# Product 3 of the output layer by seven smaller products, in chunks 3 to 7 of an attention and GELU kernel

## The chip, the cores and the metric

One core of a Trainium2 chip. The metric is the device time of one execution in microseconds; the kernel before takes 256.05 us (median of 3 runs, 256.01 to 256.41). The engines are named as the profile names them: PE (TensorE, matmuls), PEld (its weight loads), DVE (VectorE), ACT (ScalarE), POOL (GpSimd) and SP (SyncE, which only issues DMAs here).

## The reference

Linear attention over 8 batches, 8 heads, 576 positions and 64 features, then one layer with GELU:

```python
q_s = exp(q - max) / sum over the features;  k_s = exp(k - max) / sum over the positions
kv = einsum('bhsd,bhse->bhde', k_s, v)
x = einsum('bhsd,bhde->bhse', q_s, kv), heads side by side   # 4608 x 512
g = gelu(x @ w_in)                                           # 4608 x 2048
out = g @ w_out                                              # 4608 x 512
```

Inputs and output are f32 in memory. The kernel computes its matmuls in bf16 with f32 sums.

## The kernel before, in words

**Chunks.** The 4608 rows are done in nine chunks of 512. Chunks 0 to 7 are the first 512 positions of each batch; chunk 8 collects the 64 that are left of each. The loop at L1099 runs chunks 2 to 8. In each, `h_waves` (L462) computes g from x and w_in, and `y_phase` (L673; `y_last` for chunk 8) computes the output from g and w_out. Work for later chunks is put between: `next_x` (L1088) makes x of chunk c+1 and the k·v product of chunk c+2.

**Seven products instead of eight.** Both layers split their two matrices in halves both ways, and multiply sums of quarters: seven products instead of eight. In the output layer the quarters are: rows of the chunk (LO, HI: 256 each), the inner 2048 (UP, DN: 8 tiles of 128 each) and output columns (two times 256). `y_operands` (L661) lists what each of the seven multiplies. Product 3 is g[UP, LO] times (w_out[UP, right] - w_out[DN, right]); the weight difference was written over wo_bf[UP, right] before (`mix_wo`, L877). It takes 16 matmuls with 128 x 128 of g as the weights that are loaded and 256 columns of w_out moving.

**Order of y_phase.** The order in which instructions are written is the order in each engine's queue; engines meet only by semaphores. TensorE does products 4, 3, 5, 1, 2, 6, then x and k·v for later chunks, then product 7. Between them `after(i)` calls functions that the caller hooked in. ScalarE copies product 4 to `f` (`zeros32`, L706), does the exponentials of q of chunk c+2 (hook 8), copies product 3 to c12 (L709), then the exponentials of k (hook 9). VectorE subtracts product 5 from f, sums the exponentials of q (`q_sums`, L258, hook 1) and goes on with the outputs c12, c22, c11. GpSimd waits until VectorE's last sums of g are done (`touch_g`, L1083), then casts v of chunk c+2 in four pieces (L190), scales q (`q_scale`, L266) and does two adds on c22 (L732, L733). Then y is stored and the next q, k and v are loaded, all by SP's queue in this order.

**Order of h_waves.** Four groups (q = 0 to 3) of two tiles; seven products each. `x_sums` (L444) are the sums of x that products 5, 6, 7 and 4 multiply: t1 and t2 are made at the end of the y_phase before (t1 before the k·v scaling, t2 behind it), t3 and t4 within the wave, t3 just ahead of `e_sum` of groups 0 and 1. `e_sum` (L511) adds product 6 to product 5 in PSUM and frees product 7 to go on in the same bank; `r_sum` (L514) follows it. `gelu` (L517) writes g. At the end `s_parts` (L385) makes the sums of g that the output products 5, 1, 2, 6 and 7 multiply.

**Buffers.** `vf` is the f32 landing buffer of v, two in turn. `y_sb` holds the output of half a chunk, two in turn. `quad_t` holds t1 to t4. PSUM has eight banks, whose roles rotate from chunk to chunk (`turn_roles`, L456); product 3 has a bank of its own, `bx`.

Of the kernel before, what the change touches and what calls it, by code (L numbers as in the profile page):

```python
# [8 lines left out]
FP32 = mybir.dt.float32  # L9
# [7 lines left out]
def kernel(  # L17
# [16 lines left out]
    nc = tc.nc  # L34
# [53 lines left out]
    HT = M // 2  # L88
    HN = DM // 2
    w7 = singles.tile([128, HK, HN], BF16)  # L90
    s12 = singles.tile([128, HK, M], BF16)
    s5 = singles.tile([128, HK, HT], BF16)

# [10 lines left out]
    def load_main(b, name, t, parts=1):  # L104
# [5 lines left out]
        for i in range(parts):  # L110
            nc.sync.dma_start(out=f[:, i * n:(i + 1) * n, :], in_=src[:, i * n:(i + 1) * n, :])

    def load_pair(b, name, t, parts=1):
        f = f32in.tile([128, HP, NS * D], FP32, tag=name + "f")
        st[b][name + "f"] = f
        src = t[b].rearrange("h (p n) d -> (h p) (n d)", n=NS).rearrange("(x q) f -> q x f", q=128)
        n = HP // parts
        for i in range(parts):
            h0 = i * n
            if b == 0 and name == "k" and i == 0:  # L120

                nc.scalar.dma_start(out=f[:, 0, :], in_=src[:, 0, :])
                h0 = 1
            nc.sync.dma_start(out=f[:, h0:(i + 1) * n, :], in_=src[:, h0:(i + 1) * n, :])
# [8 lines left out]
    def load_v1(i):  # L133

        if i == 0:
            st[1]["vf"] = f32in.tile([128, HP, NS * D], FP32, tag="vf", name="f")
        src = v[1].rearrange("h (p n) d -> (h p) (n d)", n=NS)
        nc.sync.dma_start(out=st[1]["vf"][:, i, :], in_=src[i * 128:(i + 1) * 128, :])

# [319 lines left out]
        roles.update(bb=r["x3"], ba=r["kv1"], x0=r["bb"], x1=r["kv0"], x2=r["x0"], x3=r["ba"],  # L459
                     kv0=r["x1"], kv1=r["x2"])  # L460

    def h_waves(c, mid):  # L462

# [50 lines left out]
        def r_sum(q):  # L514
            tt(held["r", q], held["A", q], held["r", q])
# [10 lines left out]
        if mid:  # L526
            seed(1)
            mm(1, 2, 3)
            mm(2, 0, 1)
            gelu("C", 0, 1)  # L530
            mm(5, 0, 1)
            p5_copy(0, scopy)
            p5_copy(1, scopy)
            x_sums(c, (3, 4))
            seed(2, vcopy)
            seed(3, vcopy)
            mm(6, 0, 1)
# [24 lines left out]
            gelu("r", 2, 3)  # L562
            mm(3, 2, 3)
            mm(4, 2, 3)
        else:
            mm(5, 0, 1)
            seed(1)
            p5_copy(0, scopy)
            p5_copy(1, scopy)
            mm(6, 0, 1)  # L570
            x_sums(c, (3,))
            e_sum(0)
            e_sum(1)
            x_sums(c, (4,))
            mm(2, 0, 1)
            gelu("C", 0, 1)
            mm(7, 0, 1)
            r_sum(0)
            r_sum(1)
            mm(3, 0, 1)  # L580
            for q in (2, 3):
                mm(5, q)
                mm(1, q)
            mm(4, 0, 1)
            gelu("r", 0)
            gelu("B", 0, 1)
            gelu("r", 1)
            seed(2)
            seed(3)
            gelu("A", 0, 1)  # L590
            p5_copy(2, vcopy)
            p5_copy(3, vcopy)
            s_parts(c, 0, 4, (3,))
            mm(6, 2, 3)
            e_sum(2)
            e_sum(3)
            s_parts(c, 0, 4, (4,))
            mm(2, 2, 3)
            gelu("C", 2, 3)
            mm(7, 2, 3)  # L600
            r_sum(2)
            r_sum(3)
            gelu("r", 2, 3)
            mm(3, 2, 3)
            mm(4, 2, 3)
        gelu("A", 2, 3)
        gelu("B", 2, 3)
        s_parts(c, 0, 4, (0,))
        if mid:
            s_parts(c, 0, 4, (4,))  # L610
        s_parts(c, 0, 4, (2,))
        s_parts(c, 4, 4, (0,))
        s_parts(c, 4, 4, (3,))
        s_parts(c, 4, 4, (4,))
        turn_roles()
# [54 lines left out]
        }  # L670
        return act, wgt

    def y_phase(c, ins):  # L673

        act, wgt = y_operands(c)
        if c == 1:
            at = {"bd": 3, "be": 4, "bb": 0, "bx": 1, "ba": 2}
        else:  # L680
            at = {"bd": roles["x0"], "be": roles["x1"], "bb": roles["bb"], "bx": roles["x2"], "ba": roles["ba"]}
        bd, be, bb, bx, ba = (bank(at[n], "y" + n[1]) for n in ("bd", "be", "bb", "bx", "ba"))
        ysb = [moe_sb.tile([128, 2, DM], FP32, tag="y_sb", name="y_sb", bufs=2) for i in range(2)]
        c11, c12 = ysb[0][:, :, 0:HN], ysb[0][:, :, HN:DM]
        c21, c22 = ysb[1][:, :, 0:HN], ysb[1][:, :, HN:DM]
        f = zeros32

        def two(ps):
            return ps.rearrange("p (j n) -> p j n", j=2)

        def mm(m, ps, first):
            for j in range(2):
                for k in range(HK):
                    nc.tensor.matmul(  # L694
                        ps[:, j * HN:(j + 1) * HN], act[m][:, k, j * 128:(j + 1) * 128],
                        wgt[m][:, k, :], start=(first and k == 0 and j == 0),
                        stop=(k == HK - 1), skip_group_check=True,
                    )

        def after(i):  # L700
            for fn in ins.get(i, []):
                fn()

        mm(4, bd, True)
        if c > 1:
            nc.scalar.copy(out=f, in_=bd)  # L706
            after(8)
            mm(3, bx, True)
            nc.scalar.copy(out=c12, in_=two(bx))  # L709
            after(9)  # L710
        else:
            nc.vector.tensor_copy(out=f, in_=bd)
        after(0)
        mm(5, be, True)
        after(7)
        tt(f, f, be, ALU.subtract)
        after(1)
        if c > 1:
            tt(c12, c12, two(be))
        mm(1, ba, True)  # L720
        tt(c22, two(f), two(ba))
        after(2)
        mm(2, bd, False)
        nc.scalar.copy(out=c21, in_=two(bd))
        after(3)
        if c == 1:
            mm(3, be, False)
            nc.scalar.copy(out=c12, in_=two(be))
        after(4)
        mm(6, bb, True)  # L730
        tt(c22, c22, two(bb))
        tt(c22, c22, c12, eng=nc.gpsimd)  # L732
        tt(c22, c22, c21, ALU.subtract, eng=nc.gpsimd)  # L733
        after(5)
        mm(7, ba, False)
        tt(c11, two(f), two(ba))
        y_store(c, 1, ysb[1])
        y_store(c, 0, ysb[0])
        after(6)

    def y_last(c):

# [304 lines left out]
    for t in range(4):  # L1047
# [4 lines left out]
    mix_wo(1, 1)  # L1052
    mix_wo(3, 1)
    quad["r"] = wst.tile([128, 4, 2, HT], FP32, tag="w2", name="r")
    quad["t"] = wst.tile([128, 4, 2, HT], BF16, tag="w3", name="quad_t")
    h1 = {p + 3: [lambda p=p: cast_v(2, p, nc.scalar)] for p in range(HP)}
    h1[1] = [sums[0]]
    h1[3] += sums[1:3]
# [3 lines left out]
    exp_q(2, parts=2)  # L1062
    exp_k(2)

    y_phase(1, {
        0: [sums[3]],
        7: [lambda: norm_q(2, 0, 2)],
        1: [lambda: norm_q(2, 1, 2, nc.vector)],
        2: [lambda: cast_v_all(3), lambda: xbar_step(2), lambda: exp_q(3)],
        3: [lambda: kv_step(2), lambda: exp_k(3), lambda: q_sums(3)],  # L1070
        4: [lambda: table(AF.Gelu)],
        6: [lambda: load(4), lambda: x_all(2, (3, 4, 1, 5)),
            lambda: kv_step(3, lambda: x_sums(2, (1,))), lambda: x_sums(2, (2,))],
    })

    def q_late():


        nc.gpsimd.tensor_copy(out=scr[:, 2:3], in_=quad["r"][:, 0, 0, 0:1])
        q_scale(3, nc.gpsimd)  # L1080
        xbar_step(3)

    def touch_g(c):  # L1083

# [14 lines left out]
    for c in range(2, B + 1):  # L1099
        nb = c + 2  # L1100
        if 2 < c and nb < B:
            load(nb)
        elif nb == B:
            load_qrest()
        h_waves(c, q_late if c == 2 else None)
        s_parts(c, 4, 4, (2,))
        yi = {}
        if nb <= B:
            yi[8] = [lambda: exp_q(nb)]
            yi[1] = [lambda: norm_q(nb)]  # L1110
            yi[3] = [lambda: table(AF.Gelu)]
        if nb < B:
            yi[9] = [lambda: exp_k(nb)]
            yi[0] = [lambda: touch_g(c), lambda: cast_v_all(nb)]
        if c < B:
            yi[5] = [lambda: next_x(c, nb)]
            y_phase(c, yi)
        else:
            y_last(c)

# [29 lines left out]
```

## Time and profile before

| | us |
|---|---|
| median of 3 runs (range) | 256.05 (256.01 to 256.41) |
| the profiled execution, its own time | 256.13 |
| its span, first to last instruction | 254.3 |
| PE busy | 247.7 (97%) |
| DVE busy | 209.0 (82%) |
| ACT busy | 189.1 (74%) |
| POOL busy | 67.3 (26%) |
| a steady chunk, from one product 4 to the next (110.67 to 136.48 in the chain) | 25.81 |

A timeline line gives the start in us from the span's start, the duration in us, the engine, the source line, the operation, output <- inputs by the program's names, shapes, and how many were merged (x16); in brackets the idle time before it and what ended it. Merged rows last from the first start to the last end. A matmul's duration has the pipeline in it, so sixteen matmuls of 0.272 us each take 1.91 us as a row and 1.75 us in the chain, which counts from end to end. The next operation of VectorE or ScalarE starts some 0.1 us before the last one's end. The granted clock was 1.000 throughout.

### The profile page before, as it was taken

What the parts mean: (1) busy time and instruction counts of PE and PEld (TensorE: products, weight loads), DVE (VectorE), ACT (ScalarE), POOL (GpSimd) and SP (SyncE); (2) the same over time, 40 slices, a digit from 0 to 9 for tenths busy, and PEclk for the clock granted to TensorE, in tenths of its full rate; (3) what the DMA queues carried; (4) which work ended last, traced back from release to release, by engine and by line L of the source; (5) the groups of instructions that cost most, each with busy time, mean ns of one, the idle gap of its engine ahead of it and who ended that gap; (6) DMA issues with size and microseconds to landing.
All of it is one profiled execution on the core that took longest, in us unless ns stands there. A gap on an engine that the chain in (4) does not pass through costs nothing.

```text
span 254.3 us, 6526 instructions
## 1 busy us (share of the span) xinstructions
PE 247.7 (97%) x2672; PEld 195.8 (77%) x2678; DVE 209.0 (82%) x365; ACT 189.1 (74%) x321; POOL 67.3 (26%) x64
## 2 busy tenths in 40 slices
PE   7899999999999999999999999999999999999994
PEld 3444444448888888888888888888888888888883
DVE  1878799888986989897889888988898889578972
ACT  4785988699977995899689968896886787158711
POOL 1530023000735067006700580059000900040000
PEclk9999999999999999999999999999999999999999
DMA  7999999994439935980499049904830340012033
GB/s 237 400 387 425 402 406 400 398 411 174 85 125 330 266 68 131 321 340 1 109 303 377 4 85 326 378 0 86 263 71 0 84 166 3 0 55 115 1 82 86
DMA packets 43166, 50.23 MB, mean 198 GB/s; under 512 B 20224, under 2 KB 30464, under 8 KB 42880
## 3 DMA queue, kind: packets, MB, share of 16 engines
q1 hardware_dynamic: 42416, 49.13, 57.7%
q10 hardware_dynamic: 720, 0.69, 1.0%
q8 instruction: 21, 0.34, 0.6%
q14 instruction: 9, 0.07, 0.1%
HBM read 36.70 MB, written 9.44 MB: 181 GB/s over the span
## 4 chain that ended last, share of the span: by engine, by line
PE 93%; DMA 4%; ACTq 0%; issue 0%; DVE 0%; POOL 0%
PE qa L497 19%; PE ps L377 11%; PE ya L694 10%; PE qb L497 10%; PE yd L694 10%; PE ye L694 6%; PE ps L637 5%; PE qc L497 5%; PE yb L694 5%; PE yx L694 4%; PE kv L225 2%; DMA touch<-in_moe_w_in_dram 2%; DMA f<-in_v_dram 2%; PE ps L343 2%; PE ya L764 1%; PE yd L764 1%
## 5 line engine op out<-in xcount | busy, mean ns | idle before, releaser
L497 PEld LDWEIGHTS <-quad_s 128*128 128x128 bf16 x448 | 43.8, 98 | 5.3 <-issue 0.2
L694 PEld LDWEIGHTS <-g 128*128 128x128 bf16 x448 | 43.2, 98 | 5.8 <-issue 0.4
L269 POOL TENSOR_TENSOR e<-e,recq 128x2048 bf16<-128x2048 bf16 (+1 forms) x9 | 27.4, 3046 | 72.9 <-DVE recq L264 47.7
L694 PEld LDWEIGHTS <-s 128*128 128x128 bf16 x336 | 32.9, 98 | 3.8
L497 PEld LDWEIGHTS <-wi_bf 128*128 128x128 bf16 x336 | 32.8, 98 | 3.9
L497 PE MATMUL qa<-quad_t,quad_s 128*128 128x256 bf16 x224 | 29.4, 272 | 0.0
L377 PE MATMUL ps<-xT,wi_bf 128*128 128x512 bf16 x124 | 27.8, 379 | 0.2
L428 POOL TENSOR_TENSOR y_sb<-y_sb 128x512 f32<-128x512 f32 x14 | 19.5, 1390 | 24.2 <-DVE y_sb L428 21.3
L263 DVE TENSOR_REDUCE qsum<-e 128x16 f32<-128x1024 bf16 (+1 forms) x12 | 20.9, 1743 | 4.8 <-ACT e L173 4.8
L377 PEld LDWEIGHTS <-wi_bf 128*128 128x128 bf16 x128 | 12.3, 97 | 15.2 <-issue 0.5
L428 DVE TENSOR_TENSOR qb<-qa,r 128x512 f32<-128x512 f32 x28 | 18.1, 694 | 5.8 <-ACT g L521 3.1
L505 ACT COPY qc<-qa 128x512 f32<-128x512 f32 x26 | 13.9, 577 | 12.0 <-PE qa L497 11.5
L383 ACT ACTIVATE g<-ps 128x512 bf16<-128x512 f32 x32 | 17.6, 603 | 6.1 <-PE ps L377 5.8
L173 ACT ACTIVATE e<-f 128x512 bf16<-128x512 f32 (+1 forms) x42 | 20.5, 556 | 1.9 <-DMA f<-in_q_dram 1.8
L521 ACT ACTIVATE g<-r 128x512 bf16<-128x512 f32 x28 | 17.3, 631 | 6.2 <-DVE r L428 6.2
L521 ACT ACTIVATE g<-qc 128x512 bf16<-128x512 f32 x28 | 15.2, 594 | 7.7 <-PE qc L497 7.7
L428 DVE TENSOR_TENSOR r<-qa,r 128x512 f32<-128x512 f32 x28 | 18.0, 685 | 0.9 <-PE qa L497 0.7
L402 DVE TENSOR_TENSOR s<-g 128x1024 bf16<-128x1024 bf16 x28 | 18.6, 686 | 0.0
L190 POOL CAST v_aug<-f 128x576 bf16<-128x576 f32 x25 | 17.2, 723 | 3.6 <-DMA f<-in_v_dram 3.6
L178 ACT ACTIVATE ek<-f 128x2304 bf16<-128x2304 f32 (+1 forms) x10 | 17.3, 1735 | 0.5 <-DMA f<-in_k_dram 0.5
L521 ACT ACTIVATE g<-qb 128x512 bf16<-128x512 f32 x28 | 15.1, 594 | 0.7 <-PE qb L497 0.7
L497 PE MATMUL qb<-quad_t,quad_s 128*128 128x256 bf16 x112 | 15.5, 272 | 0.0
(101 smaller groups left out, 469.3 us busy)
## 6 DMA issues: line engine op xcount, KB each, us to landing
out_dram<-y_sb SPq DMA_DIRECT2D x16, 512.0 KB, 3.4
f<-in_k_dram SPq DMA_DIRECT2D x6, 1152.0 KB, 10.0
f<-in_v_dram SPq DMA_DIRECT2D x6, 1152.0 KB, 11.7
f<-in_q_dram SPq DMA_DIRECT2D x6, 1024.0 KB, 8.1
w<-in_moe_w_in_dram SPq DMA_DIRECT2D x6, 512.0 KB, 8.7
f<-in_v_dram SPq DMA_DIRECT2D x8, 288.0 KB, 6.3
f<-in_q_dram SPq DMA_DIRECT2D x4, 512.0 KB, 8.9
w<-in_moe_w_out_dram SPq DMA_DIRECT2D x2, 1024.0 KB, 12.3
```

The costliest lines, as they stand in the source:

```text
L173: nc.scalar.activation(out=dst[:, i], in_=src[:, u], func=AF.Exp)
L178: nc.scalar.activation(out=ek[b % 2][:, i:i + n], in_=st[b]["kf"][:, i:i + n].rearrange("p x (n d) -> p x n d", n=NS), func=AF.Exp,)
L190: eng.tensor_copy(out=o, in_=i)
L263: nc.vector.reduce_sum(out=qsum, in_=st[b]["eq"][:, :, i * w:(i + 1) * w, :], axis=AX.X)
L269: eng.tensor_tensor(out=e, in0=e, in1=st[b]["recq"].unsqueeze(3).to_broadcast([128, J, w, D]), op=ALU.mult,)
L377: nc.tensor.matmul(ps, wi_bf[:, dm, t * 128:(t + 1) * 128], st[c]["xT"][:, dm, :], start=(dm == 0), stop=(dm == NDM - 1),)
L383: nc.scalar.activation(out=st[c]["g"][:, t, :], in_=ps, func=AF.Gelu)
L402: tt(out=s12[:, a, half], in0=g[:, a, half], in1=g[:, b, hi], op=ALU.add)
L428: eng.tensor_tensor(out=out, in0=in0, in1=in1, op=op)
L497: nc.tensor.matmul(held[kind, q][:, u], w, mov[m][:, k], start=(m in (1, 5) and u == 0 and k == 0), stop=(k == 1), skip_group_check=True,)
L521: nc.scalar.activation(out=g[:, t:t + 2, half], in_=held[kind, q], func=AF.Gelu)
L694: nc.tensor.matmul(ps[:, j * HN:(j + 1) * HN], act[m][:, k, j * 128:(j + 1) * 128], wgt[m][:, k, :], start=(first and k == 0 and j == 0), ...
```

## The change

In chunks 3 to 7, product 3 is itself split into halves all three ways and done by seven products ("sets") of an eighth of its work. A set has four matmuls: 128 rows of g loaded as weights, 128 columns of w_out moving, over four of the eight inner tiles. Four sets add into the same PSUM bank in 128-column blocks.

- The sums of w_out that the sets need are made once, by GpSimd: two in y_phase of chunk 1, four operations in the wave of chunk 2, behind the scaling of q.
- The sums of g (`rows`, `diag`, `cols`) are made by VectorE in every chunk: three operations within the wave, behind r_sum of groups 0 and 1, three at its end, among `s_parts`, whose order changes a little.
- Sets 4, 5 and 1 go ahead of product 4; ScalarE copies their three blocks of 128 columns out (`snap`) before it copies product 4; sets 2, 3, 6 and 7 take the place of product 3 and add on the same bank.
- The blocks are put together by six GpSimd operations of 128 x 128 f32: `corner` behind the touch of g, `corner2` behind the first cast of v (it reads c12), then the three other casts of v; `spread` on c12 ahead of the adds on c22.
- v of chunks 4 to 7 has one landing buffer instead of two; the other holds the sums.
- Hooks 4 and 6 of y_phase of chunk 1 are renamed 10 and 4.

```diff
+    def v_buf(b):
+        i = b % 2 if b < 4 else 0
+        return f32in.tile([128, HP, NS * D], FP32, tag=f"vf{i}", name="f", bufs=1)
...
             r_sum(0)
             r_sum(1)
+            if sums:
+                sums(c, 0)
...
+        if sums:
+            sums(c, 1)
+        else:
+            s_parts(c, 0, 4, (0,))
...
+        def weights(self, part):
+            W = wo_bf[:, UP, HN:DM].rearrange("p (a h b) n -> p h a b n", h=2, b=2)
+            b11, b12, b21, b22 = (W[:, i, :, :, j:j + 128] for i in range(2) for j in (0, 128))
...
+            if part == 0:
+                tt(o[0], b11, b22, eng=eng)
+                tt(o[1], b12, b22, ALU.subtract, eng=eng)
+                return
+            tt(o[2], b21, b11, ALU.subtract, eng=eng)
+            tt(o[3], b11, b12, eng=eng)
+            tt(o[4], b21, b22, eng=eng)
+            w = self.w[:, 4]
+            eng.tensor_scalar(out=w, in0=w, scalar1=-1.0, scalar2=None, op0=ALU.mult)
+
+        def sums(self, c, a):
+            A = st[c]["g"][:, UP, LO]
...
+            tt(self.rows[:, o], A[:, k1], A[:, k2])
+            tt(self.diag[:, o], A[:, k1, lo], A[:, k2, hi])
+            if a:
+                s_parts(c, 0, 4, (0,))
+            tt(self.cols[:, k], A[:, k, hi], A[:, k, lo], ALU.subtract)
+            if a:
+                s_parts(c, 4, 4, (0,))
+                s_parts(c, 0, 4, (2,))
+
+        def mm(self, c, ps, sets, first):
...
+                for i, k1 in enumerate((0, 1, 4, 5)):
+                    k2 = k1 + 2
+                    lhs, rhs, r = {
+                        1: (self.diag[:, i], self.w[:, 0, i], 0),
+                        2: (self.rows[:, i, hi], W[:, k1, lo], 2),
+                        3: (A[:, k1, lo], self.w[:, 1, i], 1),
+                        4: (A[:, k2, hi], self.w[:, 2, i], 2),
+                        5: (self.rows[:, i, lo], W[:, k2, hi], 1),
+                        6: (self.cols[:, k1], self.w[:, 3, i], 3),
+                        7: (self.cols[:, k2], self.w[:, 4, i], 0),
+                    }[m]
...
+        def snap(self, ps):
+            nc.scalar.copy(out=two_d, in_=ps[:, 0:384])
+
+        def corner(self):
+            eng, d = nc.gpsimd, self.d
+            tt(d[:, 2], d[:, 2], d[:, 1], ALU.subtract, eng=eng)
+            tt(d[:, 0], d[:, 0], d[:, 2], eng=eng)
+
+        def corner2(self, o):
+            eng, d = nc.gpsimd, self.d
+            tt(d[:, 0], d[:, 0], o[:, 0, 128:HN], eng=eng)
+            tt(d[:, 0], d[:, 0], o[:, 1, 0:128], ALU.subtract, eng=eng)
+
+        def spread(self, o):
+            tt(o[:, 0, 0:128], o[:, 0, 0:128], self.d[:, 2], eng=nc.gpsimd)
+            tt(o[:, 1, 128:HN], o[:, 1, 128:HN], self.d[:, 0], eng=nc.gpsimd)
...
+        if p3:
+            p3.mm(c, bx, (4, 5, 1), True)
+            p3.snap(bx)
         mm(4, bd, True)
         if c > 1:
             nc.scalar.copy(out=f, in_=bd)
             after(8)
-            mm(3, bx, True)
+            if p3:
+                p3.mm(c, bx, (2, 3, 6, 7), False)
+            else:
+                mm(3, bx, True)
             nc.scalar.copy(out=c12, in_=two(bx))
             after(9)
...
         after(0)
+        if p3:
+            p3.corner2(c12)
+        after(6)
         mm(5, be, True)
...
         tt(c22, c22, two(bb))
+        if p3:
+            p3.spread(c12)
         tt(c22, c22, c12, eng=nc.gpsimd)
...
-        2: [lambda: cast_v_all(3), lambda: xbar_step(2), lambda: exp_q(3)],
+        2: [lambda: cast_v_all(3), first_weights, lambda: xbar_step(2), lambda: exp_q(3)],
...
         q_scale(3, nc.gpsimd)
         xbar_step(3)
+        y3.weights(1)
...
+        p3 = y3 if 2 < c < B else None
+        h_waves(c, q_late if c == 2 else None, p3 and p3.sums)
...
-            yi[0] = [lambda: touch_g(c), lambda: cast_v_all(nb)]
+            cv = [lambda hp=hp: cast_v(nb, hp, nc.gpsimd) for hp in range(HP)]
+            yi[0] = [lambda: touch_g(c)] + ([p3.corner] if p3 else []) + cv[:1]
+            yi[6] = cv[1:]
+        elif p3:
+            yi[0] = [p3.corner]
```

More of the change, by code (lines that the diff above doesn't have):

```diff
@@ L90 @@
     w7 = singles.tile([128, HK, HN], BF16)
+    two_d = singles.tile([128, 384], FP32)
     s12 = singles.tile([128, HK, M], BF16)
@@ L111, in load_main @@
             nc.sync.dma_start(out=f[:, i * n:(i + 1) * n, :], in_=src[:, i * n:(i + 1) * n, :])
+    def v_buf(b):
+        i = b % 2 if b < 4 else 0
+        return f32in.tile([128, HP, NS * D], FP32, tag=f"vf{i}", name="f", bufs=1)
     def load_pair(b, name, t, parts=1):
-        f = f32in.tile([128, HP, NS * D], FP32, tag=name + "f")
+        f = v_buf(b) if name == "v" else f32in.tile([128, HP, NS * D], FP32, tag=name + "f")
         st[b][name + "f"] = f
@@ L135, in load_v1 @@
         if i == 0:
-            st[1]["vf"] = f32in.tile([128, HP, NS * D], FP32, tag="vf", name="f")
+            st[1]["vf"] = v_buf(1)
         src = v[1].rearrange("h (p n) d -> (h p) (n d)", n=NS)
@@ L460, in turn_roles, with h_waves @@
                      kv0=r["x1"], kv1=r["x2"])
-    def h_waves(c, mid):
+    def h_waves(c, mid, sums=None):
         h_begin(c)
@@ L607, in h_waves @@
         gelu("B", 2, 3)
[L608 to L612, printed above, removed]
+        if sums:
+            sums(c, 1)
+        else:
+            s_parts(c, 0, 4, (0,))
+            if mid:
+                s_parts(c, 0, 4, (4,))
+            s_parts(c, 0, 4, (2,))
+            s_parts(c, 4, 4, (0,))
         s_parts(c, 4, 4, (3,))
@@ L671, in y_operands, with __init__ @@
         return act, wgt
-    def y_phase(c, ins):
+    class Two:
+        def __init__(self):
+            t = f32in.tile([128, 9, 512], BF16, tag="vf1", name="two", bufs=1)
+            self.w = t[:, 0:5].rearrange("p i (k n) -> p i k n", k=4)
+            self.rows = t[:, 5:7].rearrange("p i (k n) -> p (i k) n", k=2)
+            self.cols = t[:, 7:9].rearrange("p i (k n) -> p (i k) n", k=4)
+            self.diag = quad["diag"]
+            self.d = two_d.rearrange("p (i n) -> p i n", i=3)
+        def weights(self, part):
+            W = wo_bf[:, UP, HN:DM].rearrange("p (a h b) n -> p h a b n", h=2, b=2)
+            b11, b12, b21, b22 = (W[:, i, :, :, j:j + 128] for i in range(2) for j in (0, 128))
+            o = [self.w[:, i].rearrange("p (a b) n -> p a b n", b=2) for i in range(5)]
+            eng = nc.gpsimd
+            if part == 0:
[9 more added lines that the diff above has]
+            A = st[c]["g"][:, UP, LO]
+            k, k1, k2 = slice(4 * a, 4 * a + 4), slice(4 * a, 4 * a + 2), slice(4 * a + 2, 4 * a + 4)
+            o = slice(2 * a, 2 * a + 2)
+            lo, hi = slice(0, 128), slice(128, HT)
+            tt(self.rows[:, o], A[:, k1], A[:, k2])
[4 more added lines that the diff above has]
+            if a:
+                s_parts(c, 4, 4, (0,))
+                s_parts(c, 0, 4, (2,))
+        def mm(self, c, ps, sets, first):
+            A, W = st[c]["g"][:, UP, LO], wo_bf[:, UP, HN:DM]
+            lo, hi = slice(0, 128), slice(128, HT)
+            for m in sets:
+                for i, k1 in enumerate((0, 1, 4, 5)):
[9 more added lines that the diff above has]
+                    }[m]
+                    nc.tensor.matmul(
+                        ps[:, r * 128:(r + 1) * 128], lhs, rhs,
+                        start=(first and m == sets[0] and i == 0), stop=(i == 3),
+                        skip_group_check=True,
+                    )
+        def snap(self, ps):
[11 more added lines that the diff above has]
+            tt(o[:, 1, 128:HN], o[:, 1, 128:HN], self.d[:, 0], eng=nc.gpsimd)
@@ L677, in y_phase @@
+    def y_phase(c, ins, p3=None):
         act, wgt = y_operands(c)
@@ L728, in y_phase @@
             nc.scalar.copy(out=c12, in_=two(be))
-        after(4)
+        after(10)
         mm(6, bb, True)
         tt(c22, c22, two(bb))
+        if p3:
+            p3.spread(c12)
         tt(c22, c22, c12, eng=nc.gpsimd)
@@ L738, in y_phase @@
         y_store(c, 0, ysb[0])
-        after(6)
+        after(4)
     def y_last(c):
@@ L1054 @@
     quad["r"] = wst.tile([128, 4, 2, HT], FP32, tag="w2", name="r")
-    quad["t"] = wst.tile([128, 4, 2, HT], BF16, tag="w3", name="quad_t")
+    quad["t"] = wst.tile([128, 5, 2, HT], BF16, tag="w3", name="quad_t")
+    quad["diag"] = quad["t"][:, 4].rearrange("p i (k n) -> p (i k) n", k=2)
     h1 = {p + 3: [lambda p=p: cast_v(2, p, nc.scalar)] for p in range(HP)}
@@ L1063, with first_weights @@
     exp_k(2)
+    y3 = None
+    def first_weights():
+        nonlocal y3
+        y3 = Two()
+        y3.weights(0)
     y_phase(1, {
@@ L1068 @@
         1: [lambda: norm_q(2, 1, 2, nc.vector)],
-        2: [lambda: cast_v_all(3), lambda: xbar_step(2), lambda: exp_q(3)],
+        2: [lambda: cast_v_all(3), first_weights, lambda: xbar_step(2), lambda: exp_q(3)],
         3: [lambda: kv_step(2), lambda: exp_k(3), lambda: q_sums(3)],
-        4: [lambda: table(AF.Gelu)],
-        6: [lambda: load(4), lambda: x_all(2, (3, 4, 1, 5)),
+        10: [lambda: table(AF.Gelu)],
+        4: [lambda: load(4), lambda: x_all(2, (3, 4, 1, 5)),
             lambda: kv_step(3, lambda: x_sums(2, (1,))), lambda: x_sums(2, (2,))],
@@ L1104 @@
             load_qrest()
-        h_waves(c, q_late if c == 2 else None)
+        p3 = y3 if 2 < c < B else None
+        h_waves(c, q_late if c == 2 else None, p3 and p3.sums)
         s_parts(c, 4, 4, (2,))
@@ L1113 @@
             yi[9] = [lambda: exp_k(nb)]
-            yi[0] = [lambda: touch_g(c), lambda: cast_v_all(nb)]
+            cv = [lambda hp=hp: cast_v(nb, hp, nc.gpsimd) for hp in range(HP)]
[3 more added lines that the diff above has]
+            yi[0] = [p3.corner]
         if c < B:
             yi[5] = [lambda: next_x(c, nb)]
-            y_phase(c, yi)
+            y_phase(c, yi, p3)
         else:
```

## Prediction

> **What bounds the kernel now.** I read the table of engines first, then the chain of work that ended last, then the timeline of one whole chunk.
>
> ```profile
> PE 247.7 (97%) x2672; PEld 195.8 (77%) x2678; DVE 209.0 (82%) x365; ACT 189.1 (74%) x321; POOL 67.3 (26%) x64
> ```
>
> TensorE works 97% of the span. Its chain in chunk 3 has no gap, and the last product of the kernel shows a short form:
>
> ```profile
> 110.67 1.75 PE yd L694 x16
> 112.42 1.75 PE yx L694 x16
> 114.16 1.75 PE ye L694 x16
> ...
> 249.84 0.91 PE ya L764 x16
> ```
>
> Each step starts where the last ended: TensorE alone sets the time from 58 us on, so a product is worth what it takes, if nothing else becomes late. Product 3 is `yx`: 16 matmuls of 256 columns in 1.747 us, 109.2 ns each. The last line is 16 matmuls of 128 columns, each with a weight load of its own; from first start to last start they take 0.0555 us each.
>
> What could become late is read in the stretch between chunks 3 and 4:
>
> ```profile
> 119.42 3.62 POOL L269 TENSOR_TENSOR e<-e,recq 128x2048 bf16<-128x2048 bf16 x1 [1.76 <-ACT ek L178]
> ...
> 122.99 0.42 DVE L428 TENSOR_TENSOR quad_t<-xT 128x512 bf16<-128x512 bf16 x1
> 123.00 2.94 POOL L428 TENSOR_TENSOR y_sb<-y_sb 128x512 f32<-128x512 f32 x2
> ...
> 124.13 0.69 DVE L428 TENSOR_TENSOR quad_t<-xT,quad_t 128x512 bf16<-128x512 bf16 x1
> 124.74 0.67 DVE L428 TENSOR_TENSOR y_sb<-zeros,ya 128x512 f32<-128x512 f32 x1
> ...
> 125.34 0.89 DVE L428 TENSOR_TENSOR quad_t<-xT 128x512 bf16<-128x512 bf16 x1
> ...
> 125.83 1.04 PE L497 MATMUL qa<-quad_t,quad_s 128*128 128x256 bf16 x8
> 126.54 1.30 DVE L428 TENSOR_TENSOR qb<-qa,r 128x512 f32<-128x512 f32 x2 [0.31 <-PE qa L497]
> ...
> 127.58 1.04 PE L497 MATMUL qa<-quad_t,quad_s 128*128 128x256 bf16 x8
> ```
>
> The `quad_t` rows are x_sums (1), (2), (3): one shape, 0.42, 0.69 and 0.89 us. The long ones end 0.29 us after a GpSimd add ends: 124.82 after 124.53 (123.00 and the 1.53 that the first of the two shows where it is listed alone), 126.23 after 125.94. So **a VectorE operation with two inputs in SBUF waits for the GpSimd operation that is running.** It holds for the scaling of q too:
>
> ```profile
> 35.13 1.90 POOL L269 TENSOR_TENSOR e<-e,recq 128x1024 bf16<-128x1024 bf16 x1 [19.88 <-DVE recq L264]
> ...
> 36.39 1.73 DVE L269 TENSOR_TENSOR e<-e,recq 128x1024 bf16<-128x1024 bf16 x1
> ```
>
> The VectorE row ends at 38.12, 1.09 after GpSimd's 37.03; the same row started at 64.81, as GpSimd ended, takes 1.23 in all. Operations that read PSUM (0.69 f32) show no such stretch. Today x_sums (1) starts at 122.99, just as the 3.62 us scaling ends. The two e_sums (126.54) then end at 127.84, and the second half of product 7 starts at 128.02: slack 0.18. Chunk 7 has no slack:
>
> ```profile
> 203.47 1.28 DVE L428 TENSOR_TENSOR qb<-qa,r 128x512 f32<-128x512 f32 x2
> 204.21 1.19 PE L497 MATMUL qa<-quad_t,quad_s 128*128 128x256 bf16 x8
> ```
>
> 1.19 instead of 1.04: TensorE stood for 0.15.
>
> **The change, part by part.** My sum is against the profiled execution, 256.13 us (span 254.3 and 1.8 around it); the median of the runs is 256.05.
>
> *TensorE.* Seven sets of four 128-column matmuls: 28 × 0.0555 = 1.554 for 1.747. Gain 0.193 a chunk, five chunks: **-0.97**. Nearest row above: the weight load's own duration, 98 ns, if nothing hid it: 28 × 0.098 = 2.74, a loss of 1.0 a chunk. I take 55.5, since the row has just this form.
>
> The Trainium skill ("TensorE: Matmul & The Clock Gate", Back-to-back issue gap) speaks against the change: 81 ns is what it gives for sustained pairs of load and 128-column matmul, 56 only for an isolated gap. By the 81 ns, an estimate, a chunk would lose 28 × 81 - 1747 = 0.52 us. The trace's 16 pairs in a row agree with the 56; no run so far shows 28.
>
> *Waits of the new products.* Sets 5 and 1 need the sums `rows` and `diag`. VectorE comes to them at 109.84, needs about 0.34 and 0.21 by the rows of 512 and 256 elements (0.42 and 0.28, each with the next starting 0.08 before its end), and is done by 110.5; TensorE wants them at 110.73 and 110.95. The second group of sets (2, 3, 6, 7) must not write before ScalarE's snap of 384 columns has read. ScalarE is free at 112.41 (its GELU pair of 111.45 plus 0.96); between the copies of 256 (0.38) and 512 (0.58) I take 0.48, so 112.89 plus a signal; TensorE is there at 110.51 + 0.67 + 1.75 = 112.93. I cost it 0.02 a chunk, **+0.1**; each 0.1 us that the GELUs come later costs 0.1.
>
> *VectorE.* Six operations, 0.9 us in the wave and 0.9 at its end. Idle times of 0.46, 0.18 and 0.52 us take the first, the 1.16 before `zeros` (116.02) the second. Cost nothing; without that cover up to 0.9 a chunk.
>
> *GpSimd.* Six f32 operations of 128x128 a chunk. The trace has none: above it is the 128x512 add (1.33, half of the undisturbed pair of 2.67 at 224.55), below the 128x1 cast (0.19). From the bf16 rows (1.90 for 1024, 3.62 for 2048) a fixed 0.18; then 0.18 + 128 × 2.25 ns = 0.46, of which I take 0.41 from start to start. Queued behind them are three casts of v, the scaling of q and the two adds of `y_sb`. Matters of layout come to nothing: with one buffer for v from chunk 4 on, its load is issued around 129.2 + 2 and the last cast before it is over by 121. The weight sums: two in the GpSimd idle time of 2.38 before 70.77 (512 elements, 0.18 + 512 × 1.68 ns = 1.04 each), four after 80.28, with GpSimd idle until 90.43; they can hold VectorE's sums of chunk 2 for up to 0.4, whose product 5 has 0.6 slack.
>
> *What is late next.* In chunk 3's clock: product 4 now ends 0.67 later, so the f copy (112.45) starts at 113.12, the exponentials of q end at 117.2 (116.54), c12 is copied by 117.7. GpSimd's corner2 waits for c12: 117.75 to 118.6; three casts (0.62 each) to 120.45; then the scaling, **120.45 to 124.07**, where it ran 119.42 to 123.04. TensorE meanwhile is 0.19 earlier. x_sums (1) comes at about 122.95, waits to 124.07, is done at 124.36, still ahead of product 5 (124.96 - 0.19 = 124.77). After 0.81 of k·v work x_sums (2) comes at 125.09. GpSimd has done the two spreads and begins the first `y_sb` add at about 125.0. This is a tie, and it decides.
>
> If VectorE goes first, x_sums (2) is done at 125.5, in time for product 6 (125.64). x_sums (3) comes at 126.0 and waits for the add (126.58), the e_sums end at 127.5 and 128.1 where product 7 wants them at 127.39 and, with the first wait, 127.9: **+0.28**. This falls on the waves of chunks 4, 5 and 6. Chunk 7, without casts, gets the scaling 0.6 later instead of 1.0: I take +0.3 (0 to 0.5).
>
> Sum: 256.13 - 0.97 + 0.10 + 3 × 0.28 + 0.30 = 256.40, less 0.08 for the median: **256.3**.
>
> **Rivals.** A measurement of this kernel tells about 0.2%, 0.5 us, from no change.
>
> *A, the forecast: the gain is eaten by the next wave's sums.* 255.8 to 257.0, as GpSimd's small operation is 0.43 to 0.55. Chance 0.37.
>
> *B, slower: GpSimd's add goes first at the tie.* Then x_sums (2) waits to 126.33 and product 6 stands 0.98; x_sums (3) waits for the second add (127.75), the e_sums end at 128.65 and 129.25, and product 7 stands about 0.4 more: 1.4 in each of three waves. 256.05 - 0.87 + 4.2 + 0.3 = 259.7. It decides when the add takes hold before 125.09: for it, the 0.46 of an operation puts the start at 125.0; against it, the row at 123.00 took 0.2 to get going, as x_sums (1) was under way. Down to 258.5 with shorter operations. Chance 0.31.
>
> The Trainium skill ("SBUF — State Buffer", Who interferes with whom) says that whichever of the two starts first has the shared ports for the whole instruction. The rows above agree on the whole instruction; who starts first at the tie they cannot show, and by the start times alone this would be B.
>
> *C, the gain stands.* If GpSimd's operation is nearer to 0.19 than to 0.46, the scaling starts as q's sums are ready, 120.03, and the gaps between spreads and adds let x_sums through: 256.05 - 0.97 + 0.1 = 255.2, up to 255.5 with one short stall. For it: VectorE has 0.35 to 1.5 us of slack at each x_sums. Against it: even so the scaling ends 0.6 later than now, and the e_sums have 0.18. Chance 0.24.
>
> *D, 128-column matmuls do not hide their loads.* At 98 ns, 256.05 + 5 × 1.0 = 261. The row of 55.5 speaks against it. Chance 0.04. The rest (0.04) is a late cast before k·v, whose second half has 1.3 us of slack: slower.
>
> **The numbers.** Faster by over 0.2% (below 255.54): C and a little of A, 0.26. Within: most of A, 0.26. Slower: the rest of A (0.09), B, D and the cast: 0.48. Likeliest 256.3, its own range 255.8 to 257.0. For 8 in 10 the range takes in C and most of B: 255.3 to 260.0.
>
> **What would show it.** Right: 28 matmuls of 128 columns in 1.55 us; q's scaling about 1 us later against product 4's start; `quad_t` rows of 1 us and more; gaps of TensorE before L497's products 6 and 7 in chunks 4 to 7, none in chunk 3. Wrong: `quad_t` rows at 0.42 and a period of 25.6 us instead of 25.8 (C), or no gap but slow matmuls (D). A GpSimd row of 128x128 far from 0.46 moves everything.

## The result and the profile after

| | before | after |
|---|---|---|
| median of 4 runs (range), us | 256.19 (256.01 to 256.41) | 257.87 (257.78 to 258.63) |
| the profiled execution, its own time | 256.13 | 257.78 |
| its span | 254.3 | 255.7 |
| one chunk, from one product 4 or first set to the next: chunks 3, 4, 5 | 25.80, 25.76, 25.75 | 26.12, 26.20, 26.13 |
| the same, chunks 6, 7 | 25.28, 25.22 | 25.48, 25.06 |

The changed kernel takes 1.0072 of the time before (95% interval 1.005 to 1.0093): 0.7% more, where 256.3, no difference, was forecast. The time lies in the range given, above the forecast A's own range (255.8 to 257.0) and below rival B's (258.5 to 259.7). The table of engines after:

```profile
PE 248.8 (97%) x2732; PEld 195.7 (77%) x2738; DVE 221.5 (87%) x395; ACT 190.9 (75%) x326; POOL 89.8 (35%) x100
```

GpSimd has 22.5 us more work and VectorE 12.5, and TensorE is as full as before. The chain of the work that ended last (start, time from end to end, engine, tile, line) shows in chunk 3 what the small products cost, and in the wave behind it (wave 4, the wave of chunk 4) what the rest does:

```profile
110.84 0.67 PE yx L743 x12
111.51 1.75 PE yd L789 x16
113.25 0.91 PE yx L743 x16
...
125.15 1.05 PE qb L503 x8
...
127.07 0.87 PE qc L503 x8
127.94 1.15 PE qa L503 x8
```

The 28 small matmuls take 0.67 + 0.91 = 1.58 us, product 3 took 1.75. Eight matmuls of the wave take 0.87 when nothing holds them, so products 5 (125.15) and 7 (127.94) lost 0.18 and 0.28. The timeline of the same stretch says to whom:

```profile
118.01 0.99 POOL L434 TENSOR_TENSOR two_d<-two_d,y_sb 128x128 f32<-128x128 f32 x2
118.94 1.88 POOL L196 CAST v_aug<-f 128x576 bf16<-128x576 f32 x3
...
120.78 3.62 POOL L275 TENSOR_TENSOR e<-e,recq 128x2048 bf16<-128x2048 bf16 x1
...
123.13 1.56 DVE L434 TENSOR_TENSOR quad_t<-xT 128x512 bf16<-128x512 bf16 x1
...
124.80 0.29 DVE L252 TENSOR_TENSOR kvc<-kv,rec 128x128 bf16<-128x128 f32 x1
...
125.14 1.64 PEld L503 LDWEIGHTS <-quad_s 128*128 128x128 bf16 x16 [0.30 <-DVE kvc L252]
...
125.41 0.41 DVE L434 TENSOR_TENSOR quad_t<-xT,quad_t 128x512 bf16<-128x512 bf16 x1
125.49 2.88 POOL L434 TENSOR_TENSOR y_sb<-y_sb 128x512 f32<-128x512 f32 x2
...
126.34 0.90 DVE L434 TENSOR_TENSOR quad_t<-xT 128x512 bf16<-128x512 bf16 x1
...
127.90 1.19 PE L503 MATMUL qa<-quad_t,quad_s 128*128 128x256 bf16 x8
```

The scaling of q (L275) runs from 120.78 to 124.40; before it ran 119.42 to 123.04. x_sums (1), the first `quad_t` row, takes 1.56 us instead of 0.42 and ends at 124.69, 0.29 after the scaling. The two halves of the k·v scaling (`kvc`) stand behind it on VectorE, and the weight load of product 5 waited for the first of them (124.80 + 0.29 = 125.09): this product writes into the bank that the k·v scaling still reads. Before, the same row ended 1.15 ahead of product 5 (123.81, 124.96):

```profile
123.52 0.29 DVE L246 TENSOR_TENSOR kvc<-kv,rec 128x128 bf16<-128x128 f32 x1
...
124.96 1.04 PE L497 MATMUL qb<-quad_t,quad_s 128*128 128x256 bf16 x8
```

In the changed kernel, x_sums (2) then starts at 125.41, 0.08 ahead of GpSimd's add (125.49); x_sums (3) falls into that add, takes 0.90, and product 7 is late.

In the wave of chunk 7 the adds alone do it:

```profile
203.50 2.68 POOL L434 TENSOR_TENSOR y_sb<-y_sb 128x512 f32<-128x512 f32 x2
203.62 1.42 DVE L434 TENSOR_TENSOR quad_t<-xT 128x512 bf16<-128x512 bf16 x1
...
205.71 1.19 PE L503 MATMUL qa<-quad_t,quad_s 128*128 128x256 bf16 x8 [0.21 <-DVE qb L434]
```

x_sums (3) comes 0.12 after the first add and takes 1.42, and product 7 starts 0.37 late and stands 0.15 more in its middle.

### The profile page after: what moved, and what is told of

It is laid out like the page before. It is cut to its first block, busy times and chain, and to the rows that moved or that the text cites. A ratio compares the mean times of both kernels' runs of the same rounds, so it can differ in the third digit from the quotient of the medians.

```text
span 255.7 us, 6732 instructions
## 1 busy us (share of the span) xinstructions
PE 248.8 (97%) x2732; PEld 195.7 (77%) x2738; DVE 221.5 (87%) x395; ACT 190.9 (75%) x326; POOL 89.8 (35%) x100
## 4 chain that ended last, share of the span: by engine, by line
PE 83%; DVE 6%; DMA 4%; ACT 2%; issue 2%; ACTq 0%; POOL 0%; DVEq 0%
PE qa L503 19%; PE ps L383 11%; PE qb L503 10%; PE yd L789 8%; PE ya L789 7%; PE ps L648 5%; PE qc L503 4%; PE ye L789 4%; PE yb L789 3%; PE yx L743 2%; DMA f<-in_v_dram 2%; DMA touch<-in_moe_w_in_dram 2%; DVE qsum L269 2%; DVE y_sb L434 2%; PE kv L231 1%
## 5 line engine op out<-in xcount | busy, mean ns | idle before, releaser
L275 POOL TENSOR_TENSOR e<-e,recq 128x2048 bf16<-128x2048 bf16 (+1 forms) x9 | 27.4, 3046 | 49.7 <-DVE recq L270 49.1
L789 PEld LDWEIGHTS <-g 128*128 128x128 bf16 x368 | 35.2, 98 | 4.8 <-issue 0.4
L434 POOL TENSOR_TENSOR y_sb<-y_sb 128x512 f32<-128x512 f32 x14 | 18.9, 1351 | 3.7 <-issue 2.8
L408 DVE TENSOR_TENSOR s<-g 128x1024 bf16<-128x1024 bf16 x28 | 19.8, 726 | 0.0
L1201 POOL CAST scr<-g 128x1 f32<-128x1 bf16 x4 | 0.7, 187 | 49.5 <-DVE g L411 49.5
```

The costliest lines, as they stand in the source:

```text
L275: eng.tensor_tensor(out=e, in0=e, in1=st[b]["recq"].unsqueeze(3).to_broadcast([128, J, w, D]), op=ALU.mult,)
L408: tt(out=s12[:, a, half], in0=g[:, a, half], in1=g[:, b, hi], op=ALU.add)
L434: eng.tensor_tensor(out=out, in0=in0, in1=in1, op=op)
L789: nc.tensor.matmul(ps[:, j * HN:(j + 1) * HN], act[m][:, k, j * 128:(j + 1) * 128], wgt[m][:, k, :], start=(first and k == 0 and j == 0), ...
```

## The experiments

All are compared with runs of the kernel before on the same chip (medians 256.39, 256.32 and 256.47 in the three batches), with 4 to 11 runs each. "Chunk periods" run from the start of one chunk's output layer to that of the next, from chunk 3 on.

**Without the scaling.** This kernel leaves the scaling of q by its sums out in chunks 3 to 6. The theory: what the small products save stands in full, and the loss is GpSimd's scaling of q, which now runs into x_sums.

```diff
-            yi[1] = [lambda: norm_q(nb)]
+            yi[1] = [lambda: norm_q(nb) if nb < 5 else q_sums(nb)]
```

> The changed kernel, with the scaling of q by its sums left out on GpSimd in chunks 3 to 6 (the sums are still made). Theory (GpSimd holds the SBUF reads that x_sums needs): x_sums (1) takes 0.42 instead of 1.6 us, product 5 of the next wave no longer stands 0.2 to 0.3, product 7 no longer 0.28; the chunk period falls from 26.1 to about 25.65, the time from 257.9 to 255.7 (255.4 to 256.2). Rival ScalarE (product 4 and the exponentials come 0.8 later and push VectorE's queue): nothing of that is touched, so 257.5 or more. Rival VectorE (its six added sums make it late): 257.5 or more.

Measured 255.67 us (255.46 to 256.14), ratio 0.9976 (0.9967 to 0.9985). Its timeline:

```profile
123.12 0.56 DVE L434 TENSOR_TENSOR quad_t<-xT 128x512 bf16<-128x512 bf16 x1
...
124.95 1.04 PE L503 MATMUL qb<-quad_t,quad_s 128*128 128x256 bf16 x8
...
127.58 1.04 PE L503 MATMUL qa<-quad_t,quad_s 128*128 128x256 bf16 x8
```

x_sums (1) is short, products 5 and 7 come on time and run 1.04 us. The periods are 25.65, 25.60, 25.59, 24.97, 25.06: against before, 0.16 less in each chunk, and in chunk 6 another 0.15, as the old stall of product 7 is gone. So the small matmuls bring 0.16 a chunk net, and what the changed kernel has above these periods is stall: 0.47, 0.60, 0.54 and 0.51.

**Without the corner operations.** This kernel does not put product 3's blocks together. The theory: six GpSimd operations of 128 x 128 are part of what makes the scaling late, ScalarE's later exponentials the rest.

```diff
-            yi[0] = [lambda: touch_g(c)] + ([p3.corner] if p3 else []) + cv[:1]
+            yi[0] = [lambda: touch_g(c)] + cv[:1]
...
-        if p3:
-            p3.corner2(c12)
...
-        if p3:
-            p3.spread(c12)
```

> The changed kernel with the six GpSimd operations on 128x128 blocks (corner, corner2, spread) left out in chunks 3 to 7, so product 3's blocks are not put together; snap stays. Theory: the scaling of q starts as its sums are ready, near 120.2 instead of 120.8 in chunk 3's clock, x_sums (1) waits 0.6 less, the adds come 1.6 earlier; product 5 no longer stands, product 7 stands about 0.1: 256.5 (256.0 to 256.9). Rival ScalarE: the wait for the exponentials alone already makes x_sums late, and without GpSimd's operations at least two thirds of the loss stay: 257.2 or more. Rival VectorE: 257.5 or more.

Measured 256.87 us (256.49 to 257.18), ratio 1.0021 (1.0013 to 1.003). In its timeline GpSimd stands idle ahead of the scaling: this waits for ScalarE's exponentials and q's sums, and no longer for GpSimd's own queue.

```profile
120.23 3.62 POOL L275 TENSOR_TENSOR e<-e,recq 128x2048 bf16<-128x2048 bf16 x1 [1.28 <-ACT ek L184]
...
123.14 1.00 DVE L434 TENSOR_TENSOR quad_t<-xT 128x512 bf16<-128x512 bf16 x1
...
201.29 2.87 POOL L434 TENSOR_TENSOR y_sb<-y_sb 128x512 f32<-128x512 f32 x2
...
201.72 1.30 DVE L434 TENSOR_TENSOR quad_t<-xT,quad_t 128x512 bf16<-128x512 bf16 x1
...
203.08 1.05 PE L503 MATMUL qa<-quad_t,quad_s 128*128 128x256 bf16 x8 [0.27 <-DVE quad_t L434]
```

The scaling comes 0.55 earlier than in the changed kernel, 0.63 later than before against the start of y_phase. Products 5 and 6 of waves 4 to 6 come on time; only product 7 stands, and the periods are 0.17, 0.23 and 0.24 above those of the kernel without the scaling. The lines from 201 us show rival B's mechanism where the gap is wide enough: the adds start 0.43 ahead of x_sums (2), which takes 1.30, and product 6 stands 0.44. With product 7's wait, chunk 6's period is 25.83, 0.86 above that of the kernel without the scaling, where the changed kernel has 0.51. So leaving these operations out helps waves 4 to 6 and hurts wave 7.

**The k·v scaling first.** The theory: product 5 waits for the bank that the k·v scaling reads.

```diff
-            kv_step(nb, lambda: x_sums(c + 1, (1,)))
-            x_sums(c + 1, (2,))
+            kv_step(nb)
+            x_sums(c + 1, (1, 2))
```

> The changed kernel, complete, with VectorE's scaling of k.v put ahead of x_sums (1) in chunks 3 to 5 and 2. Theory: product 5 of the next wave stands for the bank that the scaling of k.v reads, which is queued behind the held x_sums (1), and not for t1 itself; in the new order the bank is free by 124.0 and t1 is ready at 124.7, before product 5 at 124.95, so the 0.2 to 0.3 there go in three waves, x_sums (2) follows at once; product 7 keeps its 0.28: 257.1 (256.8 to 257.5). If t1 itself is what product 5 waits for: no change, 257.7 to 258.0.

Measured 257.87 us (257.79 to 258.13), ratio 1.0062 (1.0049 to 1.0075): no gain. Its timeline:

```profile
125.13 1.04 PE L503 MATMUL qb<-quad_t,quad_s 128*128 128x256 bf16 x8
125.84 2.69 POOL L434 TENSOR_TENSOR y_sb<-y_sb 128x512 f32<-128x512 f32 x2
125.97 1.43 DVE L434 TENSOR_TENSOR quad_t<-xT 128x512 bf16<-128x512 bf16 x1
...
128.06 1.19 PE L503 MATMUL qa<-quad_t,quad_s 128*128 128x256 bf16 x8
```

Product 5 is on time (124.25 + 0.88), so it had been the bank. But x_sums (3) now comes 0.13 behind the add, takes 1.43, and product 7 stands 0.32 and then 0.15. The wait moved from product 5 to product 7, and the expected 257.1 was wrong: freeing the bank alone saves nothing while VectorE still has to wait for GpSimd.

**Without VectorE's sums of g.** Two kernels: the first fills their tiles with zeros by GpSimd once, the second, whose edit is shown, makes them in chunk 3 only.

```diff
-            tt(self.rows[:, o], A[:, k1], A[:, k2])
-            tt(self.diag[:, o], A[:, k1, lo], A[:, k2, hi])
+            if c == 3:
+                tt(self.rows[:, o], A[:, k1], A[:, k2])
+                tt(self.diag[:, o], A[:, k1, lo], A[:, k2, hi])
...
```

> The changed kernel with VectorE's six added sums of g (rows, diag, cols) left out in every chunk; the matmuls read zeros that are written once. Theory: VectorE's 1.8 us a chunk lie in its idle time, and GpSimd's corner2 waits for c12 anyway, so the scaling of q stays where it is and the time stays within 0.4 of the changed kernel: 257.5 to 257.9. Rival VectorE: the loss goes, 256.3 or less. Rival ScalarE: 257.5 to 257.9.

> The changed kernel with VectorE's six added sums of g made in chunk 3 only; chunks 4 to 7 multiply what is left there. Theory: as the sums lie in VectorE's idle time, 257.4 to 257.9. Rival VectorE: the loss goes, 256.4 or less. e4_no_gsums had the same aim, but its fills of zero by GpSimd held VectorE's sums in chunk 2 and cost 1.4 us once.

The first took 259.79 us (259.6 to 260.64), ratio 1.0142 (1.0126 to 1.0157), and tells nothing of the sums: GpSimd's fills of 128x1024 in chunk 2 (1.84 us for two, from 80.46) put the weight sums later, one of VectorE's `s` rows (L399) grew to 1.64 us, product 5 waited 1.35 for the next, and chunk 2 alone became 1.4 longer. The second took 257.93 (257.67 to 258.23), ratio 1.0064 (1.0052 to 1.0076): within the scatter of these runs, the six sums cost nothing.

**The kernel before with the operations alone.** Six GpSimd operations of 128x128 f32 on a tile of their own, where the change has them; then also two ScalarE copies of 384 columns behind the f copy, so that the exponentials come 0.8 us later.

```diff
+            yi[0] = [lambda: touch_g(c)] + x + cv[:1] + x + cv[1:]
...
+                for _ in range(2):
+                    nc.scalar.copy(out=two_s, in_=bd[:, 0:384])
```

> The kernel before, complete, with six GpSimd operations of 128x128 f32 on a scratch tile in chunks 3 to 7, where the change has its own: two ahead of the first cast of v, two behind it, two ahead of the adds on c22. Nothing waits for c12 here, so the scaling of q starts only 0.1 later (119.5 instead of 119.4), but the adds come 1.1 later. Theory: x_sums (1) waits 0.1, x_sums (3) 0.2 to 0.5 longer than before, and with 0.18 of slack product 7 stands 0 to 0.3 in waves 4 to 7: 256.7 (256.2 to 257.5). If GpSimd's operations do nothing by themselves: within 0.2 of the kernel before.

> As the last one, and ScalarE gets two more copies of 384 columns behind its f copy, so that the exponentials of q come 0.8 later, as they do in the changed kernel. TensorE's products are those of before. Theory: the scaling runs from about 120.2 to 123.8, x_sums (1) waits 0.7, the adds come 1.8 later, and products 5 to 7 of the next wave stand 0.3 to 1.0 in waves 4 to 6: 257.7 (257.0 to 259.5), so the loss comes back without any change of the matmuls. If the loss lies in the new matmuls or in VectorE's sums of g: within 0.4 of the kernel before.

The first took 256.27 us (256.1 to 257.58), ratio 1.0002 (0.9991 to 1.0014), where 256.7 was expected: no loss on balance. In chunk 3 the scaling comes 0.14 later and no product waits. In chunk 5 it comes 1.04 later (172.02 for 170.98), for another reason: the adds end later, so the store of y and the loads behind it on SP's queue do too, and the first cast of v waits 0.94 for its transfer. There x_sums (1) takes 1.38 and product 7 loses 0.21; in return the old stall of 0.15 in wave 7 is gone. The second took 258.22 (257.3 to 259.5), ratio 1.0072 (1.005 to 1.0093), but does not prove the sum of the two: its runs spread over 2.2 us, the profiled one (257.54) lost 0.44 ahead of chunk 3, and of the rest 0.75, almost nothing (0.03 each) fell on waves 4 and 5. In chunk 3 the scaling started 9.83 us after the start of y_phase, and TensorE, without the small products, came to product 5 later by what these save. In chunk 5 of this run, too, the cast of v waited 1.06 for its transfer; in the changed kernel no cast of chunks 3 to 5 shows such a wait. So these two runs are no clean test of lateness alone.

**The scaling in the next wave.** q of chunks 5 to 8 is scaled behind x_sums (4), where VectorE mostly reads PSUM. Once with TensorE's order altered as well (product 4 ahead of the sets, product 5 between them), once with the late scaling alone, once with that order alone; in all three, the sums of g stand at the wave's end.

```diff
             x_sums(c, (4,))
+            if 3 < c < B:
+                scale_late(c)
...
-        if p3:
-            p3.mm(c, bx, (4, 5, 1), True)
-            p3.snap(bx)
         mm(4, bd, True)
         if c > 1:
             nc.scalar.copy(out=f, in_=bd)
+            if p3:
+                p3.mm(c, bx, (4, 5, 1), True)
+                p3.snap(bx)
             after(8)
             if p3:
+                mm(5, be, True)
                 p3.mm(c, bx, (2, 3, 6, 7), False)
```

> The changed kernel, complete, reordered: q of chunks 5 to 8 is scaled in the next wave, behind x_sums (4), where VectorE works from PSUM; product 4 goes ahead of the sets, product 5 between them; all six sums of g are made at the end of the wave; corner and corner2 go ahead of the casts of v. Theory: x_sums (1) to (3) meet only the two adds, as in the kernel before, products 5 to 7 do not stand, and TensorE's gain stands: 255.4 (255.0 to 256.0), below both kernels. Rival VectorE (its queue at the end of the wave, 1 us longer, makes the y phase late) or a late q for its transposition: 256.5 or more.

> The changed kernel with two edits: q of chunks 5 to 8 is scaled in the next wave behind x_sums (4), and all six sums of g stand at the wave's end. TensorE's order is that of the changed kernel (sets 4, 5, 1, then product 4), so ScalarE's f copy and the exponentials stay 0.84 us late, and the corner operations stay between the casts. Theory (the loss comes only where the 3.62 us scaling holds x_sums; ScalarE's delay in itself costs nothing): 255.7 us (255.4 to 256.1), products 5 to 7 of waves 4 to 6 without a gap, chunk periods 25.6. Rival (the early product 4 is what repaired the reordered kernel): 257.3 or more.

> The changed kernel with TensorE's order alone altered: product 4 ahead of sets 4, 5, 1, product 5 between these and sets 2, 3, 6, 7, sums of g at the wave's end, the three casts behind the corner operations; q is scaled where the changed kernel scales it. ScalarE's exponentials then come 0.5 us later than in the kernel before (the snap) where the changed kernel has 0.84. Theory (what counts is when the scaling ends): it ends some 0.35 earlier than in the changed kernel, 9.8 us after the start of y_phase, product 5 no longer stands, product 7 still does by 0.1 to 0.3 in waves 4 to 6: 256.8 us (256.3 to 257.3). Rival (the order of the products is the whole repair): 255.7.

Both together: 255.62 us (255.5 to 255.84), ratio 0.9973 (0.9961 to 0.9985). The late scaling alone: 255.95 (255.5 to 256.28), ratio 0.9984 (0.9975 to 0.9993). The intervals overlap, so these two are not told apart; both are faster than either kernel. The timeline of the second of them:

```profile
125.05 1.04 PE L508 MATMUL qb<-quad_t,quad_s 128*128 128x256 bf16 x8
...
127.67 1.04 PE L508 MATMUL qa<-quad_t,quad_s 128*128 128x256 bf16 x8
...
128.46 3.62 POOL L275 TENSOR_TENSOR e<-e,recq 128x2048 bf16<-128x2048 bf16 x1
```

Products 5 and 7 come on time, and the periods of the first three chunks are 25.65, 25.59, 25.60, those of the kernel without the scaling. Chunk 6 keeps a stall, with a period of 25.32 against 24.97 there: the adds start at 199.42, x_sums (2) comes at 201.07, takes 1.30, and product 6 stands 0.36.

The order alone: 260.27 us (260.18 to 260.31), ratio 1.0151 (1.0137 to 1.0165), where 256.8 was expected. Its timeline:

```profile
118.25 0.99 POOL L434 TENSOR_TENSOR two_d<-two_d,y_sb 128x128 f32<-128x128 f32 x2
119.19 2.49 POOL L196 CAST v_aug<-f 128x576 bf16<-128x576 f32 x4
...
121.64 3.62 POOL L275 TENSOR_TENSOR e<-e,recq 128x2048 bf16<-128x2048 bf16 x1
...
123.20 2.34 DVE L434 TENSOR_TENSOR quad_t<-xT 128x512 bf16<-128x512 bf16 x1
...
126.00 1.05 PE L503 MATMUL qb<-quad_t,quad_s 128*128 128x256 bf16 x8 [0.72 <-DVE kvc L252]
```

The expectation of a start at 9.8 us failed on two counts: q's sums came only 0.11 earlier against the start of y_phase (117.48 - 110.85 for 117.41 - 110.67), and they did not decide, since this edit also put all four casts behind corner2, where the changed kernel has one ahead of it. That is another 0.62 before the scaling, which started 10.79 us after y_phase; x_sums (1) took 2.34, and product 5 stood 0.88. So the run is a test of a later scaling, and not of an earlier one as planned. The table sets the four kernels that have the small products and the scaling side by side: when the scaling starts after the start of y_phase (chunk 3), the period behind it, and what this is above the 25.65 of the kernel without the scaling:

| | scaling starts, us after y_phase | period | lost |
|---|---|---|---|
| no corner operations | 120.23 - 110.69 = 9.54 | 25.82 | 0.17 |
| the change | 120.78 - 110.67 = 10.11 | 26.12 | 0.47 |
| the order alone | 121.64 - 110.85 = 10.79 | 26.80 | 1.15 |
| late scaling alone | 17.70 | 25.65 | 0.00 |

From the first row to the second the scaling starts 0.57 later and 0.30 is lost; from the second to the third 0.68 later, and the chunk is 0.68 longer. Chunk 4 says the same of the last two: 0.59 later, 0.61 longer. So once the slack is used up, the whole delay is lost. The altered order itself costs nothing: with it and the late scaling the period is 25.62.

## Why the prediction was right in its mechanism and short in its size

The profiled executions differ by 257.78 - 256.13 = 1.65 us. By the periods: the small products bring 5 x 0.16 = -0.79; stalls in waves 4 to 6 cost 0.47 + 0.60 + 0.54 = 1.61, and wave 7 0.51 less the old 0.15 = 0.36; chunk 3's output layer starts 0.17 later (110.84 against 110.67 in the chain); 257.78 - 255.7 = 2.08 lies outside the span instead of 1.83. Together 1.60.

- **TensorE: right.** Forecast -0.97 and +0.10 for the snap, so 0.173 a chunk; 0.16 measured. Small loads hide in the real stream too: the second sixteen take 0.91 us, about 57 ns each. Rival D is out, and with it the 81 ns that the Trainium skill ("TensorE: Matmul & The Clock Gate", Back-to-back issue gap) gives for sustained pairs: for these 28, with larger matmuls between the groups, the trace does not bear it out.
- **VectorE's sums: right**, at nothing: without them in four of five chunks the time is 257.93, with them 257.87.
- **GpSimd's small operations: right in size, a little short in place.** One takes 0.46 (median of the ten of corner, 459 ns; 544 for spread, under VectorE's work), as estimated; but the second of a pair reads what the first writes, and a pair lasts 0.99, 0.53 from start to start instead of 0.41. (The two spreads, of which neither reads what the other writes, last 0.87 together where nothing disturbs them, as in the late scaling alone.) The forecast also let corner2 follow c12 at once, while the first cast of v held GpSimd until 118.05. The scaling starts at 10.11 instead of 9.94.
- **The lock: right.** x_sums (1) ended 0.29 after the scaling, as the rows of before say. Of the Trainium skill's rule ("SBUF — State Buffer", Who interferes with whom) the rows shown here agree with the part on the whole instruction: x_sums ended only after the GpSimd operation that had started before it.
- **The tie: VectorE was first**, by 0.07 to 0.08 us, in each of waves 4 to 6. So A, not B. It was less of a tie than the forecast took it for. Once x_sums (1) has waited, both queues go on from the end of the scaling: x_sums (2) starts 1.00 to 1.01 behind it, the add 1.08 to 1.09, in these waves and in wave 4 of the kernel before with the added operations and of the altered order alone. The forecast had 1.02 and 0.93: it took 0.46 for each of the two spreads, and the first lasted 0.64. B's mechanism is real all the same: without the corner operations, and with the late scaling, it showed in the wave of chunk 7, at 0.44 and 0.36.
- **Product 7 and wave 7: right**, 0.28 for the forecast 0.28, and 0.36 for 0.30. The first has some luck in it: the first e_sum ended 0.35 later than forecast (127.85 for 127.5), and product 7's turn came 0.38 later (127.77 for 127.39), so the two errors cancel. For wave 7 the forecast named a size and no order of events.
- **The step that failed: "x_sums (1) ... is done at 124.36, still ahead of product 5".** It asked only whether product 5 had its operand. Behind x_sums (1) on VectorE stood the k·v scaling, and product 5 needs the bank that this reads. Before, the first `kvc` row ended 1.15 us ahead of product 5, so no view of before named that wait. In the trace of the change it makes up the 1.61 - 3 x 0.28 = 0.77 us that waves 4 to 6 lost beyond the forecast: product 5 starts some 0.18, 0.32 and 0.25 late. It is not 0.77 that could have been saved at this place, as the run with the k·v scaling first shows: there product 5 is on time, and product 7 loses as much instead.
- **Not foreseen:** 0.25 outside the span and 0.17 ahead of chunk 3. The time outside the span is 1.7 to 1.9 in the kernel before, 2.1 to 2.2 in the changed one, 1.8 without the corner operations and 1.9 to 2.1 with the late scaling alone; no run isolates why, and the cause stays open. The 0.17 is there already at the first product of the output layer (58.26 for 58.09), ahead of any added operation, and the twelve profiles spread over 57.97 to 58.43 at this point. So nothing shows that it belongs to the change.

The sum again: 256.40 + 0.77 + 0.08 (a smaller gain) + 0.06 (wave 7) + 0.17 + 0.25 = 257.73, for 257.78.

## What to carry to other kernels

Work taken off the engine that sets the time is only kept if the engines that feed its next stage do not get later by more than their slack; here 0.16 us a chunk was won, and a 3.62 us GpSimd operation that came 1.2 us later cost three times that. When an instruction is going to wait, follow everything queued behind it to its readers and to the banks that it frees, not only its own result. If a long operation holds a shared resource, move it to a stretch where the other engine does not need that resource: here this turned a loss of 0.7% into a gain of 0.2 to 0.3%.

## What the runs showed of the hardware that was not expected

- In back-to-back GpSimd operations a waiting VectorE operation gets in at the boundary: x_sums (3) at 126.34 took 0.90, ended at 127.24, while the two adds ran on from 125.49 to 128.37. The pair of adds takes 2.61 us where no such VectorE operation comes (70.77 before), 2.67 where one waits at its boundary (224.55 before, which the forecast took for undisturbed), and 2.88 here, where x_sums (2) had also started 0.08 ahead: the first add then lasts 1.46 instead of 1.26.
- GpSimd's weight sums of 128x512 in bf16 took 1.16 us each where 1.04 was estimated from the scaling rows, and the multiplication by -1 of the same size 1.49. They lay in idle time.
